# One-token attention with a feed-forward branch on one core: w2 split evenly, products in halves of a tile, one matmul for the queries, one store for the result

## The chip, the cores and the metric

One core of one Trainium2 chip runs the kernel. The metric is the device time of one execution in microseconds (us), lower is better; a time is the median of several runs. The profiler gives a span, from the first to the last instruction, which is a little shorter than the device time of the same execution. Engines are called by the short names of the profile: PE is TensorE (its weight loads are PEld), DVE is VectorE, ACT is ScalarE, POOL is GpSimd, SP is SyncE. A name with a q (SPq, ACTq) is the engine's instruction queue, which issues DMAs.

## The reference

Four tokens, one per batch entry, each go through layer normalisation, then through an attention with cached keys and values and, beside it, through a feed-forward block. Both results are added to the input. Everything is float32.

```python
B, Sq, D = 4, 1, 512;  H, Sk, Dh = 32, 4096, 128;  F = 1792
def _A_ref(x, k_cache, v_cache, wq, wo):          # caches: (B, H, Sk, Dh)
    q = (x @ wq).reshape(B, Sq, H, Dh).transpose(0, 2, 1, 3)
    scores = jnp.einsum("bhqd,bhkd->bhqk", q, k_cache) * (Dh ** -0.5)
    p = jax.nn.softmax(scores, axis=-1)
    o = jnp.einsum("bhqk,bhkd->bhqd", p, v_cache)
    return o.transpose(0, 2, 1, 3).reshape(B, Sq, H * Dh) @ wo
def _B_ref(x, w1, w2):
    return jnp.einsum("bsf,fd->bsd", jax.nn.silu(jnp.einsum("bsd,df->bsf", x, w1)), w2)
xn = _layernorm(x)
return x + _A_ref(xn, k_cache, v_cache, wq, wo) + _B_ref(xn, w1, w2)
```

The two caches hold 268 MB each. They are read once; wq and wo are 8.4 MB each, w1 and w2 3.7 MB each.

## The kernel before

**Tiles.** The caches are cut into T = 32 tiles each: a tile is one batch entry b and G = 4 heads, in SBUF as 128 partitions by R = 128 rows of Dh = 128 numbers (65,536 bytes a partition, 8.4 MB). Each head takes 32 partitions, and each partition 128 consecutive positions of the cache. Two buffers (`k_t`) hold K tiles, one (`v_t`) holds a V tile. The buffers are used for other things at both ends: the first `k_t` serves as scratch for x and w1, the first `v_t` holds wq; at the end `k_t` also takes the last V tile and then w2, and `v_t` takes wo. All loads are issued by SP, in order, so that a load that must wait for its buffer holds up those behind it.

**The head** (lines 84 to 283). x is normalised; the feed-forward's hidden layer (w1, SiLU) is computed on PE and ACT and turned so that the hidden units lie on the partitions (`ht_sb`). The hidden layer has 1792 = 14 x 128 units. The kernel treats them as FC = 13 full pieces of 128 units on 128 partitions and FX = 4 pieces of HP = 32 units on 32 partitions (`hp_x`, `h_x`, `hx_sb`). The hidden units are spread out with zeros between them (`OS` = 8 columns each) so that a later matmul fills 32 output partitions. Then q is computed from wq (L245, L259) into `q_h`, heads on the partitions. `queries(n)` (L270) spreads the queries of four heads over the 128 partitions with four matmuls of 32 rows each, once for every four tiles.

**The loop** runs over the 32 tiles i (L364 to L386). For each tile:

- `products` (L285), called for each quarter of STEP = 32 rows: DVE multiplies K by the query, in place (L291); POOL adds the upper half of each row to the lower (L295), for POOL_ROWS = 32 rows of a quarter, in the last quarter for 16.
- `sums` (L302): DVE adds up the rows: those that POOL halved (L307) and those that it left whole (L306).
- `maxima` (L309): DVE finds the greatest score of each head with two reductions, two transposes of 32x32 blocks and one multiply by the scale (L317).
- `softmax` of the tile before (L321): four exponentials on ACT.
- `values` of the tile before (L330): 32 matmuls on PE, in the trace 64 instructions, of the probabilities with V.
- `heads_out` of the tile before (L345): ACT copies the result from PSUM (L349), DVE multiplies it by a mask (L352) and adds four columns into one (L356), PE adds it into the row of all heads (L357).

`tc.issue_after` holds the next tile's first products behind the maxima, and the queries' matmuls behind the V matmuls. The scheduler of the language sets the semaphores; each engine runs its instructions in the order of the program.

**The end** (L389 to L450). SP issues wo in two loads and w2 in pieces, cut at the numbers W2_CUTS. w2's 13 full pieces go to 128 partitions, in four loads with 7, 4, 1 and 1 rows of w2 for each; the other 128 rows of w2 go to 32 partitions, four rows each, in four loads of 64 KB to every fourth partition (L402). The last tile's `softmax`, `values` and `heads_out` follow. The heads' results are divided by the sums of the exponentials (L418), turned (L423, L428) and multiplied with wo, 32 matmuls in the loop at L437, which goes on with w2's first seven pieces and the four small ones. ACT copies these sums to SBUF (L441). `accumulate` (L155 to L161) adds them, and the products with w2's other pieces, into `acc`, where x already is: four matmuls each, one for 128 of the 512 output columns, into 32 partitions each. DVE copies `acc` (L447), and two DMAs, one issued by SP and one by ACT (L450), store 8 rows of 128 numbers each.

Of the kernel before, what the change touches and what calls it, by code (L numbers as in the profile page):

```python
# [20 lines left out]


@with_exitstack
def kernel(
# [67 lines left out]
    h_x = scratch[:, 5 * D + DC * F : 5 * D + DC * F + HP]  # L92
# [12 lines left out]
    nc.gpsimd.memset(h_x, 0.0)  # L105
    nc.vector.memset(xpad, 0.0)
    p_t = const.tile([P, R, G], F32, name="p_t")
    nc.gpsimd.memset(p_t, 0.0)
# [37 lines left out]
        own, pick.rearrange("p (r g) -> p r g", r=NR), axis=AX, op=ALU.add  # L146
    )


    OS = PH // B  # L150
    fold = const.tile([P, B, OS], F32, name="fold")
    nc.gpsimd.memset(fold, 0.0)
    nc.vector.tensor_copy(fold[:, :, 0], pick[:, :B])

    def accumulate(lhsT, rhs, start=False, stop=False):  # L155

        for j in range(D // P):
            nc.tensor.matmul(  # L158
                acc[PH * j : PH * (j + 1), :], lhsT, rhs[:, j * P : (j + 1) * P],
                start=start, stop=stop,  # L160
            )  # L161

    accumulate(fold[:B].rearrange("p b s -> p (b s)"), x_sb, start=True)


    nmean = const.tile([B, 1], F32, name="nmean")
# [26 lines left out]

    hp = ps_s.tile([P, FT * P], F32, name="sm")
    hp_x = ps_s.tile([P, HP], F32, name="sm")
    w1_f = w1_t[:, :, : FC * P].rearrange("p c (m f) -> p c f m", f=FC)
    w1_x = w1_t[:, :, FC * P :].rearrange("p c (m f) -> p c f m", f=FX)  # L200
# [13 lines left out]
    for j in range(4):  # L214
        rows, n = slice(32 * j, 32 * j + B), FN[j] * P
        nc.scalar.activation(h_sb[rows, :n], hp[rows, :n], AF.Silu)
        nc.scalar.activation(h_x[rows, :], hp_x[rows, :], AF.Silu)
    hx_ps = ps_q.tile([HP, FX, B], F32, name="q_ps")
    nc.tensor.matmul(  # L219
        hx_ps, h_x, ident.rearrange("p (j m) -> p j m", j=FX)[:, :, :B], start=True, stop=True  # L220
    )
    hx_sb = const.tile([HP, FX, B], F32, name="hx_sb")
    nc.vector.tensor_copy(hx_sb, hx_ps)  # L223
    ht_ps = ps_s.tile([P, FT, 4, B], F32, name="sm")
    for t in range(FT):
        nc.tensor.matmul(
# [5 lines left out]
    ht_sb = const.tile([P, FT, 4, B, OS], F32, name="ht_sb")  # L232
    nc.gpsimd.memset(ht_sb, 0.0)
    nc.vector.tensor_copy(ht_sb[:, :, :, :, 0], ht_ps)
    hT = [ht_sb[:, t, j] for j in range(4) for t in range(FN[j])]


    NM = H // G // 4
    qp = ps_s.tile([P, G * Dh], F32, name="sm")
# [23 lines left out]
                start=True, stop=True,  # L263
            )
    q_h = const.tile([P, B, Dh], F32, name="q_h")
    nc.vector.tensor_copy(q_h, qh_ps)  # L266

    q_ps, vs, st = {}, {}, {}

    def queries(n):  # L270

        t = ps_q.tile([P, B, Dh], F32, name="q_ps")
        for g in range(G):
            rows = slice(g * PH, (g + 1) * PH)
            k = g * PH + PH // 4 * (n // NM) + n % NM
            nc.tensor.matmul(  # L276
                t[rows].rearrange("p b d -> p (b d)"),
                ident[rows, k : k + 1].to_broadcast([PH, PH]),
                q_h[rows].rearrange("h b d -> h (b d)"),
                start=True, stop=True,  # L280
            )
        for b in range(B):
            q_ps[n * B + b] = t[:, b, :]

# [23 lines left out]

    def maxima(i):  # L309

        nc.vector.tensor_reduce(m_t[:, :1], st[i], axis=AX, op=ALU.max)  # L311
        mt = small.tile([P, PH], F32, name="mt", bufs=1)
        nc.vector.transpose(mt, m_t)  # L313
        gm = small.tile([P, 1], F32, name="gm", bufs=1)
        nc.vector.tensor_reduce(gm, mt, axis=AX, op=ALU.max)
# [3 lines left out]
        return nb, nc.vector.transpose(nb, mb).ins  # L319

    def softmax(i, nb):  # L321
        s = st.pop(i)
        for g in range(G):
            rows = slice(g * PH, (g + 1) * PH)
            nc.scalar.activation(  # L325
                p_t[rows, :, g], s[rows, :], AF.Exp, bias=nb[rows, :1], scale=scale,
                accum_out=l_t[rows, i % B, i // B, g : g + 1],
            )

# [15 lines left out]
    def heads_out(i):  # L345

        h, b = i // B * G, i % B
        o_sb = small.tile([P, NR, Dh], F32, name="o_sb", bufs=1)
        nc.scalar.activation(  # L349
            o_sb.rearrange("p r d -> p (r d)"), o_ps, AF.Copy  # L350
        )
        nc.vector.tensor_tensor(  # L352
            o_sb, o_sb, own[:, :, None].to_broadcast([P, NR, Dh]), op=ALU.mult
        )
        o_1 = small.tile([P, Dh], F32, name="o_1", bufs=1)
        nc.vector.tensor_reduce(o_1, o_sb.rearrange("p r d -> p d r"), axis=AX, op=ALU.add)  # L356
# [34 lines left out]
    w2_x = w2_t[:HP, FC * D : (FC + FX) * D]  # L391
    w2_t = w2_t[:, : FC * D].rearrange("p (f n) -> p f n", f=FC)
    src_x = w2[FC * P :].rearrange("(p e) n -> p (e n)", p=HP)
    for t, w, n, cuts in ((wo_t, wo, H, WO_CUTS), (w2_t, w2[: FC * P], FC, W2_CUTS)):
# [19 lines left out]
        )  # L414
    rl = const.tile([H, B], F32, name="rl")
    nc.vector.reciprocal(rl, ls_ps)
    o_row = const.tile([H, B, Dh], F32, name="o_row")
# [4 lines left out]
    for n in range(NQ):  # L422
# [4 lines left out]
    ot = const.tile([P, H, B], F32, name="ot")  # L427
    nc.vector.tensor_copy(ot, ot_ps.rearrange("p b c -> p c b"))  # L428

    part = ps_q.tile([P, D], F32, name="q_ps")  # L430
    nc.vector.memset(part, 0.0)
    rows = [(ot[:, c, :], wo_t[:, c, :]) for c in range(H)]
    rows += [(hT[f][:, :, 0], w2_t[:, f, :]) for f in range(W2_CUTS[0])]
    rows += [(hx_sb[:, e, :], w2_x[:, e * D : (e + 1) * D]) for e in range(FX)]
    for c, (a, w) in enumerate(rows):
        j = 32 * (c % 4)
        nc.tensor.matmul(  # L437
# [1 line left out]
        )  # L439
    part_sb = small.tile([P, NR * Dh], F32, name="o_sb", bufs=1)  # L440
    nc.scalar.activation(part_sb, part, AF.Copy)  # L441
    accumulate(fold.rearrange("p b s -> p (b s)"), part_sb)
    for f in range(W2_CUTS[0], FC):
        accumulate(hT[f].rearrange("p b s -> p (b s)"), w2_t[:, f, :], stop=(f == FC - 1))

    res = small.tile([P, P], F32, name="s")
    nc.vector.tensor_copy(res, acc)  # L447
    of = of.rearrange("b (j n) -> j b n", j=D // P)
    for k, eng in enumerate((nc.sync, nc.scalar)):
        eng.dma_start(of[2 * k : 2 * k + 2], res[k * P // 2 : (k + 1) * P // 2 : OS, :])  # L450


# [30 lines left out]
```

## Time and profile before

| what | value |
|---|---|
| device time, median of 3 runs | 1306.87 us (1306.11 to 1307.1) |
| device time of the profiled execution | 1306.47 us |
| span of the profiled execution | 1304.5 us |
| DVE busy | 974.5 us (75%), 541 instructions |
| POOL busy | 511.5 us (39%), 145 instructions |
| PE busy (matmuls) | 357.1 us (27%), 2518 instructions |
| ACT busy | 92.8 us (7%) |
| bytes moved by DMA | 561.42 MB, 430 GB/s over the span |
| mean granted clock of PE | 0.629 |

The busy tenths of the page cut the span into 40 slices of 32.6 us; a 9 stands for 90% or more. A group of the page is one line of the code on one engine: the shapes out and in, the count, the total and the mean, and then how long the engine stood idle just before those instructions and what ended it. A timeline row gives the start, the length, the engine, the line, the operation and the count of merged instructions. A stretch gives busy time by engine in the order PE, PEld, DVE, ACT, POOL, then the clock granted to PE, the busy share of the 16 DMA engines and the rate in GB/s. Shares of short stretches can pass 1, because a packet is booked where it ends.

### The profile page before, as it was taken

The page shows a single profiled execution, that of the slowest core. Times are in us where ns is not written, and L with a number is a line of the kernel's source. Part 1 is how long each engine was busy: PE and PEld are TensorE (multiplying, and loading weights), DVE is VectorE, ACT ScalarE, POOL GpSimd, SP SyncE. Part 2 cuts the span into 40 slices and gives each one's busy share as a digit, 9 for nine tenths or more (in the row PEclk, how much of TensorE's full clock was granted, in tenths as well). Part 3 has the DMA queues.
Part 4 walks back from the last instruction along what each step waited for, and adds up shares of the span by engine and source line. Part 5 has one row for each costly group of instructions (what it writes and reads, how often), then busy time and mean ns, then how long its engine had stood idle before and what let it go on. Part 6 is the DMA issues. An engine that isn't in the chain of part 4 may idle for free.

```text
span 1304.5 us, 6383 instructions
## 1 busy us (share of the span) xinstructions
PE 357.1 (27%) x2518; PEld 87.1 (7%) x2518; DVE 974.5 (75%) x541; ACT 92.8 (7%) x301; POOL 511.5 (39%) x145
## 2 busy tenths in 40 slices
PE   4321232221123321133322132332123232212227
PEld 1000000000000000000000000000000000000001
DVE  1499777887777797777797777788777779777770
ACT  1010000000000000000000000000000000000000
POOL 0255333444333444332444433344433344433340
PEclk9655666655666665666665566665566666566668
DMA  9999999999999999999999999999999999999997
GB/s 402 449 421 446 422 445 424 443 426 442 427 437 432 435 434 434 435 432 437 432 433 436 432 435 432 437 430 439 430 439 428 441 426 443 424 444 425 440 423 327
DMA packets 10490, 561.42 MB, mean 430 GB/s; under 512 B 1192, under 2 KB 1208, under 8 KB 1468
## 3 DMA queue, kind: packets, MB, share of 16 engines
q1 hardware_dynamic: 10450, 561.01, 99.4%
q8 instruction: 20, 0.33, 0.1%
q14 instruction: 10, 0.08, 0.0%
q10 hardware_dynamic: 10, 0.00, 0.0%
HBM read 561.00 MB, written 0.01 MB: 430 GB/s over the span
## 4 chain that ended last, share of the span: by engine, by line
DMA 73%; PE 18%; DVE 7%; POOL 1%; issue 0%; SPq 0%; ACT 0%; POOLq 0%; DVEq 0%; ACTq 0%
DMA v_t<-in_A_v_cache_dram 53%; PE o_ps L336 17%; DMA k_t<-in_A_k_cache_dram 15%; DVE k_t L291 4%; DMA k_t<-in_B_w_dram 3%; DVE s L307 2%; DMA v_t<-in_A_wq_dram 2%; POOL k_t L295 1%; PE sm L245 1%; DVE s L306 1%; PE q_ps L437 0%; PE acc L158 0%; DVE m_t L311 0%; DVE mt L313 0%; ACT o_sb L441 0%
## 5 line engine op out<-in xcount | busy, mean ns | idle before, releaser
L295 POOL TENSOR_TENSOR k_t<-k_t 128x2048 f32<-128x2048 f32 (+1 forms) x128 | 508.6, 3984 | 745.6 <-DVE k_t L291 745.6
L291 DVE TENSOR_TENSOR k_t<-k_t,q_ps 128x4096 f32<-128x4096 f32 x128 | 562.3, 4413 | 222.9 <-DMA k_t<-in_A_k_cache_dram 222.9
L336 PE MATMUL o_ps<-v_t,p_t 128*16 128x512 f32 x1984 | 286.0, 741 | 824.6 <-DMA v_t<-in_A_v_cache_dram 824.6
L307 DVE TENSOR_REDUCE s<-k_t 128x32 f32<-128x2048 f32 (+1 forms) x128 | 257.6, 2013 | 11.5 <-POOL k_t L295 11.5
L336 PEld LDWEIGHTS o_ps<-v_t,p_t 128*16 128x16 f32 x1984 | 66.6, 113 | 1026.1 <-issue 945.9
L349 ACT ACTIVATE o_sb<-o_ps 128x512 f32<-128x512 f32 x32 | 19.1, 597 | 1097.0 <-issue 1081.4
L306 DVE TENSOR_REDUCE s<-k_t 128x16 f32<-128x2048 f32 x32 | 72.8, 2276 | 0.0
L325 ACT ACTIVATE p_t<-s,nb 32x128 f32<-32x128 f32 x128 | 66.5, 519 | 16.9 <-DVE nb L319 13.4
L352 DVE TENSOR_TENSOR o_sb<-o_sb,own 128x512 f32<-128x512 f32 x32 | 21.8, 680 | 28.1 <-ACT o_sb L349 27.9
L357 PE MATMUL o_all<-o,w_t 128*32 128x128 f32 x64 | 15.6, 332 | 88.4 <-DVE o L356 88.4
L356 DVE TENSOR_REDUCE o<-o_sb 128x128 f32<-128x512 f32 x32 | 32.7, 1023 | 3.2
L325 ACT ACTIVATION_READ_ACCUMULATOR p_t<-s,nb 32x1 f32 x128 | 25.5, 199 | 0.0
L357 PEld LDWEIGHTS o_all<-o,w_t 128*32 128x32 f32 x64 | 4.8, 116 | 117.8 <-DVE o L356 117.8
L447 DVE COPY s<-acc 128x128 f32<-128x128 f32 x1 | 0.3, 292 | 14.8 <-PE acc L158 14.8
L336 PE MATMUL o_ps<-k_t,p_t 128*16 128x512 f32 x64 | 9.0, 724 | 7.6 <-DMA k_t<-in_A_v_cache_dram 7.6
L245 PE MATMUL sm<-v_t,xpad 128*32 128x512 f32 x64 | 9.9, 786 | 1.0 <-DMA v_t<-in_A_wq_dram 1.0
L311 DVE TENSOR_REDUCE m_t<-s 128x1 f32<-128x128 f32 x32 | 9.1, 284 | 1.1
L223 DVE COPY hx_sb<-q_ps 32x16 f32<-32x16 f32 x1 | 0.2, 163 | 12.4 <-PE q_ps L219 12.4
L319 DVE STREAM_TRANSPOSE nb<-mb 128x32 f32<-128x32 f32 x32 | 6.8, 211 | 3.3
L437 PE MATMUL q_ps<-v_t,ot 128*4 128x512 f32 x64 | 8.8, 701 | 0.4 <-DVE ot L428 0.4
L276 PE MATMUL q_ps<-q_h,ident 32*32 32x512 f32 x64 | 8.5, 599 | 0.8 <-DVE q_h L266 0.8
L255 DVE COPY o_sb<-sm 128x512 f32<-128x512 f32 x1 | 0.7, 691 | 10.6 <-PE sm L245 10.6
(85 smaller groups left out, 77.1 us busy)
## 6 DMA issues: line engine op xcount, KB each, us to landing
v_t<-in_A_wo_dram SPq DMA_DIRECT2D x2, 4096.0 KB, 25.4
k_t<-in_B_w_dram SPq DMA_DIRECT2D x1, 3584.0 KB
k_t<-in_B_w_dram SPq DMA_DIRECT2D x1, 1792.0 KB
k_t<-in_B_w_dram SPq DMA_DIRECT2D x1, 1024.0 KB, 27.2
k_t<-in_A_k_cache_dram SPq DMA_DIRECT2D x32, 48.2
k_t<-in_B_w_dram SPq DMA_DIRECT2D x2, 256.0 KB, 13.6
v_t<-in_A_v_cache_dram SPq DMA_DIRECT2D x31, 28.9
k_t<-in_B_w_dram SPq DMA_DIRECT2D x4, 64.0 KB
```

The costliest lines, as they stand in the source:

```text
L245: nc.tensor.matmul(qp[32 * j : 32 * j + 32, :], xpad[:, c, a : a + PH], wq_t[:, c, n * G * Dh : (n + 1) * G * Dh], start=(m == 0 and c == ...
L291: nc.vector.tensor_tensor(k[:, a:z, :], k[:, a:z, :], q[:, None, :].to_broadcast([P, STEP, Dh]), op=ALU.mult)
L295: nc.gpsimd.tensor_tensor(k[:, a:v, :half], k[:, a:v, :half], k[:, a:v, half:], op=ALU.add)
L306: nc.vector.tensor_reduce(s[:, v:z], k[:, v:z, :], axis=AX, op=ALU.add)
L307: nc.vector.tensor_reduce(s[:, a:v], k[:, a:v, :half], axis=AX, op=ALU.add)
L311: nc.vector.tensor_reduce(m_t[:, :1], st[i], axis=AX, op=ALU.max)
L325: nc.scalar.activation(p_t[rows, :, g], s[rows, :], AF.Exp, bias=nb[rows, :1], scale=scale, accum_out=l_t[rows, i % B, i // B, g : g + 1],)
L336: last = nc.tensor.matmul(o[j : j + NR * G, :], p_t[:, rows, :].rearrange("p r g -> p (r g)"), v[:, rows, :].rearrange("p r d -> p (r d)") ...
L349: nc.scalar.activation(o_sb.rearrange("p r d -> p (r d)"), o_ps, AF.Copy)
L352: nc.vector.tensor_tensor(o_sb, o_sb, own[:, :, None].to_broadcast([P, NR, Dh]), op=ALU.mult)
L356: nc.vector.tensor_reduce(o_1, o_sb.rearrange("p r d -> p d r"), axis=AX, op=ALU.add)
L357: nc.tensor.matmul(o_all[:, b, :], w_t[:, W0 - h : W0 - h + H], o_1, start=False, stop=(i == T - 1))
```

## The change

- STEP is 64 instead of 32 rows, so that `products` is called twice a tile; POOL halves 64 rows of the first half and 48 of the second. The halved and whole rows of a tile stay 112 and 16.
- q is multiplied by minus the scale when it is copied (`q_h`); the maxima become minima, and the multiply by the scale falls away. Nine DVE instructions a tile remain in the loop.
- `heads_out` multiplies and adds on POOL, in three instructions, instead of on DVE in two.
- `queries` is one matmul with 128 rows, against a table `spread`, which POOL writes at the head with two copies.
- The hidden layer is 14 full pieces of 128 units; the 32-partition pieces, the zeros between columns and the products with them fall away. w2 is loaded in four loads to all 128 partitions, with 7, 4, 2 and 1 rows each. None of them waits for an earlier load any more (before, the last three did, because of the number of loads in flight).
- `accumulate` writes 4 partitions in each of the four blocks of 32, instead of 32. The result is brought into 4 partitions by four copies, on DVE and ACT in turn, and stored by one DMA of SP.
- Some tiles share buffers: `o_row`, `ot` and `res` take those of `o_sb` and `s`.

```diff
-STEP = 32
-POOL_ROWS = 32
-POOL_ROWS_LAST = 16
+STEP = 64
+POOL_ROWS = 64
+POOL_ROWS_LAST = 48
-W2_CUTS = (7, 11, 12)
+W2_CUTS = (7, 11, 13)
...
-    FX = 4
-    HP = 32
-    FC = (F - HP * FX) // P
+    FC = F // P
...
-                acc[PH * j : PH * (j + 1), :], lhsT, rhs[:, j * P : (j + 1) * P],
+                acc[32 * j : 32 * j + B, :], lhsT, rhs[:, j * P : (j + 1) * P],
...
-        for j in range(FX):
-            nc.tensor.matmul(
-                hp_x[32 * j : 32 * j + B, :], xnT[:, c, :], w1_x[:, c, j, :],
-                start=(c == 0), stop=(c == DC - 1),
-            )
...
-    nc.vector.tensor_copy(q_h, qh_ps)
+    nc.vector.tensor_scalar_mul(q_h, qh_ps, -scale)
+    spread = const.tile([P, H // G, G, PH], F32, name="spread")
+    rows = ident.rearrange("p (g j m) -> p j g m", g=G, j=4)
+    for m in range(NM):
+        nc.gpsimd.tensor_copy(
+            spread.rearrange("p (j m) g i -> p m j g i", m=NM)[:, m],
+            rows[:, :, :, m, None].to_broadcast([P, 4, G, PH]),
+        )
...
-        for g in range(G):
-            rows = slice(g * PH, (g + 1) * PH)
-            k = g * PH + PH // 4 * (n // NM) + n % NM
-            nc.tensor.matmul(
-                t[rows].rearrange("p b d -> p (b d)"),
-                ident[rows, k : k + 1].to_broadcast([PH, PH]),
-                q_h[rows].rearrange("h b d -> h (b d)"),
-                start=True, stop=True,
-            )
+        nc.tensor.matmul(
+            t.rearrange("p b d -> p (b d)"),
+            spread[:, n].rearrange("p g i -> p (g i)"),
+            q_h.rearrange("h b d -> h (b d)"),
+            start=True, stop=True,
+        )
...
-        nc.vector.tensor_reduce(m_t[:, :1], st[i], axis=AX, op=ALU.max)
+        nc.vector.tensor_reduce(m_t[:, :1], st[i], axis=AX, op=ALU.min)
...
-        mb = small.tile([P, PH], F32, name="mb", bufs=1)
-        nc.vector.tensor_scalar_mul(mb, gm.to_broadcast([P, PH]), -scale)
...
-        nc.vector.tensor_tensor(
+        nc.gpsimd.tensor_tensor(
             o_sb, o_sb, own[:, :, None].to_broadcast([P, NR, Dh]), op=ALU.mult
         )
-        o_1 = small.tile([P, Dh], F32, name="o_1", bufs=1)
-        nc.vector.tensor_reduce(o_1, o_sb.rearrange("p r d -> p d r"), axis=AX, op=ALU.add)
+        nc.gpsimd.tensor_tensor(o_sb[:, :2, :], o_sb[:, :2, :], o_sb[:, 2:, :], op=ALU.add)
+        o_1 = o_sb[:, 2, :]
+        nc.gpsimd.tensor_tensor(o_1, o_sb[:, 0, :], o_sb[:, 1, :], op=ALU.add)
...
-            if z == W2_CUTS[0]:
-                for q in range(4):
-                    nc.sync.dma_start(w2_x[q::4, :], src_x[q::4, :])
...
-    rows += [(hT[f][:, :, 0], w2_t[:, f, :]) for f in range(W2_CUTS[0])]
-    rows += [(hx_sb[:, e, :], w2_x[:, e * D : (e + 1) * D]) for e in range(FX)]
+    rows += [(hT[:, f, :], w2_t[:, f, :]) for f in range(W2_CUTS[0])]
...
-    res = small.tile([P, P], F32, name="s")
-    nc.vector.tensor_copy(res, acc)
-    of = of.rearrange("b (j n) -> j b n", j=D // P)
-    for k, eng in enumerate((nc.sync, nc.scalar)):
-        eng.dma_start(of[2 * k : 2 * k + 2], res[k * P // 2 : (k + 1) * P // 2 : OS, :])
+    res = small.tile([P, NR * Dh], F32, name="o_sb", bufs=1)[:B]
+    for j in range(D // P):
+        src, dst = acc[32 * j : 32 * j + B, :], res[:, j * P : (j + 1) * P]
+        if j % 2 == 0:
+            nc.vector.tensor_copy(dst, src)
+        else:
+            nc.scalar.activation(dst, src, AF.Copy)
+    nc.sync.dma_start(of, res)
```

More of the change, by code (lines that the diff above doesn't have):

```diff
@@ L104 @@
     nc.gpsimd.memset(h_sb, 0.0)
-    nc.gpsimd.memset(h_x, 0.0)
     nc.vector.memset(xpad, 0.0)
@@ L147 @@
     )
[L150 to L153, printed above, removed]
     def accumulate(lhsT, rhs, start=False, stop=False):
@@ L158, in accumulate @@
             nc.tensor.matmul(
-                acc[PH * j : PH * (j + 1), :], lhsT, rhs[:, j * P : (j + 1) * P],
+                acc[32 * j : 32 * j + B, :], lhsT, rhs[:, j * P : (j + 1) * P],
                 start=start, stop=stop,
             )
-    accumulate(fold[:B].rearrange("p b s -> p (b s)"), x_sb, start=True)
+    accumulate(ident[:B, :B], x_sb, start=True)
     nmean = const.tile([B, 1], F32, name="nmean")
@@ L197 @@
     hp = ps_s.tile([P, FT * P], F32, name="sm")
-    hp_x = ps_s.tile([P, HP], F32, name="sm")
-    w1_f = w1_t[:, :, : FC * P].rearrange("p c (m f) -> p c f m", f=FC)
-    w1_x = w1_t[:, :, FC * P :].rearrange("p c (m f) -> p c f m", f=FX)
+    w1_f = w1_t.rearrange("p c (m f) -> p c f m", f=FC)
     for c in range(DC):
@@ L216 @@
         nc.scalar.activation(h_sb[rows, :n], hp[rows, :n], AF.Silu)
-        nc.scalar.activation(h_x[rows, :], hp_x[rows, :], AF.Silu)
-    hx_ps = ps_q.tile([HP, FX, B], F32, name="q_ps")
-    nc.tensor.matmul(
-        hx_ps, h_x, ident.rearrange("p (j m) -> p j m", j=FX)[:, :, :B], start=True, stop=True
-    )
-    hx_sb = const.tile([HP, FX, B], F32, name="hx_sb")
-    nc.vector.tensor_copy(hx_sb, hx_ps)
     ht_ps = ps_s.tile([P, FT, 4, B], F32, name="sm")
@@ L231 @@
         )
[L232 to L235, printed above, removed]
+    hT = const.tile([P, FC, B], F32, name="hT")
+    for j in range(4):
+        z = F0[j] + FN[j]
+        nc.vector.tensor_copy(hT[:, F0[j] : z, :], ht_ps[:, : FN[j], j, :])
     NM = H // G // 4
@@ L325, in softmax @@
             nc.scalar.activation(
-                p_t[rows, :, g], s[rows, :], AF.Exp, bias=nb[rows, :1], scale=scale,
+                p_t[rows, :, g], s[rows, :], AF.Exp, bias=nb[rows, :1], scale=-1.0,
                 accum_out=l_t[rows, i % B, i // B, g : g + 1],
@@ L390 @@
     w2_t = kpool.tile([P, R, Dh], F32, name="k_t").rearrange("p r d -> p (r d)")
-    w2_x = w2_t[:HP, FC * D : (FC + FX) * D]
     w2_t = w2_t[:, : FC * D].rearrange("p (f n) -> p f n", f=FC)
-    src_x = w2[FC * P :].rearrange("(p e) n -> p (e n)", p=HP)
-    for t, w, n, cuts in ((wo_t, wo, H, WO_CUTS), (w2_t, w2[: FC * P], FC, W2_CUTS)):
+    for t, w, n, cuts in ((wo_t, wo, H, WO_CUTS), (w2_t, w2, FC, W2_CUTS)):
         w = w.rearrange("(p f) n -> p f n", p=P)
@@ L416 @@
     nc.vector.reciprocal(rl, ls_ps)
-    o_row = const.tile([H, B, Dh], F32, name="o_row")
+    o_row = small.tile([P, NR, Dh], F32, name="o_sb", bufs=1)[:H]
     nc.vector.tensor_tensor(
@@ L426 @@
         )
-    ot = const.tile([P, H, B], F32, name="ot")
+    ot = small.tile([P, P], F32, name="s").rearrange("p (c b) -> p c b", b=B)
     nc.vector.tensor_copy(ot, ot_ps.rearrange("p b c -> p c b"))
```

11 lines of the change are left out of this document (4 added, 7 removed).

## The prediction

> **What bounds the kernel now.** I began with the page: the busy tenths by slice, the DMA queues, the chain's shares, and the group of the widest VectorE instruction.
>
> ```profile
> DVE  1499777887777797777797777788777779777770
> ...
> DMA  9999999999999999999999999999999999999997
> GB/s 402 449 421 446 422 445 424 443 426 442 427 437 432 435 434 434 435 432 437 432 433 436 432 435 432 437 430 439 430 439 428 441 426 443 424 444 425 440 423 327
> ...
> q8 instruction: 20, 0.33, 0.1%
> ...
> L291 DVE TENSOR_TENSOR k_t<-k_t,q_ps 128x4096 f32<-128x4096 f32 x128 | 562.3, 4413 | 222.9 <-DMA k_t<-in_A_k_cache_dram 222.9
> ```
>
> The DMA row is full in every slice but the last, at some 434 GB/s, while VectorE, the busiest engine, stands idle 222.9 us waiting for K. So the loop is a stream of 561 MB that nothing interrupts. Next the timeline of one tile from the middle, to see how far the engines are from interrupting it:
>
> ```profile
> 563.93 0.33 SPq L83 DMA_DIRECT2D v_t<-in_A_v_cache_dram  x1
> ...
> 564.35 0.38 SPq L83 DMA_DIRECT2D k_t<-in_A_k_cache_dram  x1
> ...
> 573.67 8.75 DVE L291 TENSOR_TENSOR k_t<-k_t,q_ps 128x4096 f32<-128x4096 f32 x2 [7.24 <-DMA k_t<-in_A_k_cache_dram]
> ...
> 593.10 8.87 PE L336 MATMUL o_ps<-v_t,p_t 128*16 128x512 f32 x64 [25.98 <-DMA v_t<-in_A_v_cache_dram]
> ...
> 600.23 1.21 DVE L307 TENSOR_REDUCE s<-k_t 128x16 f32<-128x1024 f32 x1
> ...
> 602.02 0.33 SPq L83 DMA_DIRECT2D v_t<-in_A_v_cache_dram  x1
> ```
>
> The K load issued at 564.35 stands behind a V load that takes until 592.96, so K could be issued some 28 us later and the stream would not notice. A V load is issued 9 us after the one before landed, while about 19 us of K is queued: 10 us of slack. VectorE works from 573.67 to 601.44 on a tile (27.8 us), and a pair of tiles lasts 38.6 us. Nothing in the loop sets the end but the stream's own rate, and this change keeps its bytes. What can move is the end. Its timeline:
>
> ```profile
> 1281.23 0.60 ACT L349 ACTIVATE o_sb<-o_ps 128x512 f32<-128x512 f32 x1 [16.96 <-issue]
> ...
> 1281.86 0.69 DVE L352 TENSOR_TENSOR o_sb<-o_sb,own 128x512 f32<-128x512 f32 x1 [17.10 <-ACT o_sb L349]
> 1282.58 1.02 DVE L356 TENSOR_REDUCE o<-o_sb 128x128 f32<-128x512 f32 x1
> ...
> 1286.43 8.76 PE L437 MATMUL q_ps<-v_t,ot 128*4 128x512 f32 x64 [0.38 <-DVE ot L428]
> 1295.71 1.90 PE L437 MATMUL q_ps<-k_t,ht_sb 128*4 128x512 f32 x14 [0.52 <-DMA k_t<-in_B_w_dram]
> 1297.54 1.04 PE L437 MATMUL q_ps<-k_t,hx_sb 32*4 32x512 f32 x8
> 1298.69 0.60 ACT L441 ACTIVATE o_sb<-q_ps 128x512 f32<-128x512 f32 x1 [16.86 <-PE q_ps L437]
> ...
> 1301.14 0.29 DVE L447 COPY s<-acc 128x128 f32<-128x128 f32 x1 [14.77 <-PE acc L158]
> 1301.46 0.59 SPq L450 DMA_DIRECT2D out_dram<-s  x1
> 1301.47 1.42 ACTq L450 DMA_DIRECT2D out_dram<-s  x1
> ```
>
> PE reaches the first piece of w2 only 0.5 us before it has landed: TensorE's serial work and the stream arrive together. The last view is the stretches of half a microsecond there (length, busy of each engine, clock, DMA share, GB/s):
>
> ```profile
> 1295.00:1295.50 0.50, 0.19 (x4) 0.00 (x0) 0.00 (x0) 0.00 (x0) 0.00 (x0) 1.00 0.83 340
> ...
> 1297.50:1298.00 0.50, 0.50 (x11) 0.10 (x8) 0.00 (x0) 0.00 (x0) 0.00 (x0) 1.00 0.25 102
> ...
> 1299.50:1300.00 0.50, 0.50 (x24) 0.50 (x20) 0.00 (x0) 0.00 (x0) 0.00 (x0) 1.00 0.12 45
> ```
>
> The share falls away over 5 us instead of at once: some DMA engines end early, a few late. The landing marks that each of the 16 leaves behind every load say the same: the spread between first and last is 0.74 us at the first load and 4.92 us at the last V (1267.16 and 1272.08). The last piece of w2 lands at 1300.55.
>
> **The change part by part**, against the profiled execution (span 1304.5, time 1306.47, which is 0.40 below the median 1306.87).
>
> *Halves of a tile, nine VectorE instructions, the scale moved into q, the maximum's multiply dropped: 0.* The elements are the same: 128 rows multiplied, 112 halved by GpSimd as before (64+48 against 3x32+16). From K's landing: two multiplies of 2 x 4.33 (17.4); GpSimd's first half 9.05, from 8.8 to 17.9; sum of 64 halved rows 4.4 (22.3); 16 whole rows 2.2 (24.5); GpSimd's 48 rows, 4.52 + 2.37 less one start of 0.2, end at 24.6; their sum 3.4 (28.0). That is 0.2 later than now, with 28 us of cover; without cover it would cost 32 x 0.2 = 6 us. The 0.18 us multiply (L317) and 1.7 us (L352, L356) leave VectorE, which is idle anyway: 0.
>
> *Queries by one matmul: 0.* The nearest row is L130, 128x512, two instructions, 1.92 us, against 1.06 for the four quarters now. It follows the V matmuls, whose last one already released the next V load, and 26 us of waiting for V hide it. The two GpSimd copies that build the spread table run near 3 us, long before q (45 us).
>
> *The head without the extra w2 rows and the padded w1 product: 0.* It ends before wq lands (31.25).
>
> *heads_out on GpSimd: in the loop 0, at the end +1.1.* In the loop its three instructions follow the tile's last half and have about 10 us until the next. At the end they stand in the chain. GpSimd's rows: 128x2048 4.524, 128x1024 2.367, so 2.106 ns an element and 0.21 a start: 512, 256 and 128 elements take 1.29 + 0.75 + 0.48 = 2.52, plus three hops of 0.12 (VectorE to GpSimd at 1004.63): 2.88 against 1.77 now (1281.83 to 1283.60). Ends: +0.2 (896 elements, no starts but one hop) and +3.0 (twice the rate an element, since these are other shapes). I take +1.1, whose rows are the same operation.
>
> *164 TensorE instructions fewer: the last V lands 0.45 earlier.* 34 products of the padded rows and 48 of the queries go, each a weight load and a matmul. In the trace, instruction blocks of 16 KB arrive every 76 us or so, and the first, ninth and seventeenth (32.9, 597.0, 1178.0) are followed by steps of about 1.0 us in the spread of landings; the eighteenth (1255.7) raises it from 4.41 to 4.92 just ahead of the last V. 164 instructions at some 134 a tile of 38.6 us are 47 us, so this block comes after the last V: -0.45. Ends: 0, and -0.9 if other engines' blocks also miss the slowest one. [...]
>
> *w2 even over the partitions.* wo's 64 matmuls now end at 1295.2; they will end at 1295.2 + 1.1 - 0.45 = 1295.85. The first piece (1295.66) has landed by then: the wait of 0.48 is absorbed. 14 matmuls take 1.90 where 22 took 2.91: -1.01. ScalarE as before. Then 64 instead of 56 matmuls of L158, at 1.78/56 = 0.032: +0.25. Together TensorE ends 1.1 - 0.45 - 0.48 - 1.01 + 0.25 = -0.59, at 1300.5. The stream: each of the four 64 KB loads is marked by 8 DMA engines only, the latest ones among them, and takes these 1.2 us (a packet of 8 KB is 0.31); spread over 16 the last piece lands 0.6 earlier, near 1300.0, and its 8 matmuls would end at 1300.3. So TensorE decides, by 0.2.
>
> *Result in 4 partitions: +0.9.* All four copies write one tile, and each waits for the one before across engines. A copy of 128 columns on VectorE is 0.29; on ScalarE 0.25 (between 4x32 at 0.17 and 4x384 at 0.48); three hops of 0.04: 1.20 against 0.29. Ends: +0.3 (pairs side by side) and +1.4 (ScalarE at 0.48).
>
> *One store: -0.36.* ScalarE's store needs 1.42 us of issue and its mark comes at 1303.50, SyncE's at 1303.14. Without ScalarE's the end follows SyncE's. Ends: 0 and -0.6 (a plain load's issue is 0.33, not 0.59).
>
> **Sum**: -0.59 + 0.9 - 0.36 = -0.05: 1306.4 by the profiled execution, 1306.8 as a median.
>
> **The rivals.**
> *The end chain is longer (slower).* GpSimd's three instructions in the last heads_out at twice the rate: +1.9 on the sum, 1308.7, and 1309.0 with the copies at their upper end. Any excess over 0.05 makes it slower than before; for it: no row has GpSimd at these shapes; against: two shapes on one line.
> *The blocks' move gains nothing (a little slower).* If another DMA engine is then as late, V lands at 1272.08 as now, and the sum is 1306.8 + 0.45 = 1307.3. For it: ten blocks of 8 KB of the other engines' instructions also arrive, on engines that the trace does not name. Against: at the load after V the second-latest mark is 0.53 us ahead of the last.
> *The end is shorter (faster).* Copies in pairs, the blocks' -0.9 and a 0.33 us issue: -1.1 or so, 1305.7. No less than 1305.3: the last piece's landing near 1300 and the store's 3 us stand behind any work.
> *The halves stop overlapping (slower).* If GpSimd waited for both multiplies, a tile would take 17.4 + 15.7 + 10 + 1 = 44 us against 38.6, and the loop 32 x 5.5 = 176 us more: 1483. It decides once a tile passes 38.6. Against it: GpSimd starts at 578.22 inside VectorE's 573.67 to 582.42 today.
> *VectorE bound the loop after all (faster).* 1.9 us fewer a tile would give 32 x 1.9 = 61 us: 1246. Against: its 222.9 us of idling for K.
>
> **How the numbers follow.** Forecast, the trade at the end: 60 in 100, 1305.8 to 1308.0. Blocks without gain 12, longer end 13, shorter end 11, no overlap 2, VectorE 2. Within 0.2% (2.6 us, about what a measurement tells from no change) lie the first two, 8 of the longer and 8 of the shorter end: 0.88. Slower: 0.07, 5 of the longer end and the lost overlap. Faster: 0.05, 3 of the shorter end (something at the head or the stream that I have not seen) and VectorE. The predicted time is 1306.8. The bounds of the parts, joined as independent, give -1.2 and +2.1: 1305.5 to 1308.9; 0.2 more below for the spread of runs.
>
> **What would show it.** Pairs of V landings still 38.6 us apart; VectorE idle for K, more than 222.9 us by some 60; GpSimd's last three at 2.5 us; no wait of TensorE for w2's first piece; four copies in a row before the store; the spread of landings under 4.9 at the last V. Wrong would be a gap in the DMA row within the loop, an end chain that waits for w2's last piece, or copies side by side.

## The result and the profile after

The changed kernel takes 1309.89 us, the median of 11 runs (1308.99 to 1311.55); the kernel before, on the same chip, 1306.87 (11 runs, 1306.11 to 1308.33). The ratio is 1.0025, with a 95% interval of 1.0016 to 1.0035: slower by 3.0 us. The profiled execution took 1310.83 us with a span of 1309.1, which is 4.4 and 4.6 us more than before's. Its page first:

```profile
DMA  9999999999999999999999999999999999999997
GB/s 403 445 431 435 431 435 437 427 441 425 437 429 435 433 431 435 431 435 429 437 431 433 433 435 431 435 431 437 431 433 433 433 431 441 425 439 427 437 423 300
...
q8 instruction: 19, 0.31, 0.1%
...
L270 DVE TENSOR_TENSOR k_t<-k_t,q_ps 128x8192 f32<-128x8192 f32 x64 | 553.1, 8684 | 298.4 <-DMA k_t<-in_A_k_cache_dram 298.4
```

The loop is still a stream: no gap in the DMA row, and VectorE idles for K 298.4 us, 75 more than before. One tile pair from the middle, as a timeline:

```profile
555.78 8.84 PE L314 MATMUL o_ps<-v_t,p_t 128*16 128x512 f32 x64 [25.42 <-DMA v_t<-in_A_v_cache_dram]
...
575.01 17.29 DVE L270 TENSOR_TENSOR k_t<-k_t,q_ps 128x8192 f32<-128x8192 f32 x2 [9.90 <-DMA k_t<-in_A_k_cache_dram]
583.78 15.53 POOL L274 TENSOR_TENSOR k_t<-k_t 128x4096 f32<-128x4096 f32 x2 [15.97 <-DVE k_t L270]
...
594.50 9.95 PE L314 MATMUL o_ps<-v_t,p_t 128*16 128x512 f32 x64 [26.23 <-DMA v_t<-in_A_v_cache_dram]
```

GpSimd starts on the first half while VectorE multiplies the second, and the V matmuls of two tiles start 38.72 us apart, where it was 38.64 before: over 32 tiles that is some 2.5 us. Nothing in the loop interrupts the DMA. Then the end:

```profile
1274.33 9.67 PE L314 MATMUL o_ps<-k_t,p_t 128*16 128x512 f32 x64 [6.55 <-DMA k_t<-in_A_v_cache_dram]
...
1284.83 1.04 POOL L330 TENSOR_TENSOR o_sb<-o_sb,own 128x512 f32<-128x512 f32 x1 [17.55 <-ACT o_sb L327]
1285.95 0.72 POOL L333 TENSOR_TENSOR o_sb<-o_sb 128x256 f32<-128x256 f32 x1
1286.75 0.45 POOL L335 TENSOR_TENSOR o_sb<-o_sb 128x128 f32<-128x128 f32 x1
...
1288.66 2.07 PE L396 MATMUL sm<-o_sb,up 32*128 32x128 f32 x8 [0.77 <-DVE o_sb L391]
...
1291.11 9.80 PE L409 MATMUL q_ps<-v_t,s 128*4 128x512 f32 x64 [0.38 <-DVE s L401]
...
1300.74 1.89 PE L409 MATMUL q_ps<-k_t,hT 128*4 128x512 f32 x14
...
1305.40 0.28 DVE L423 COPY o_sb<-acc 4x128 f32<-4x128 f32 x1 [14.34 <-PE acc L147]
...
1306.33 0.27 ACT L425 ACTIVATE o_sb<-acc 4x128 f32<-4x128 f32 x1 [0.35 <-DVE o_sb L423]
1306.63 0.29 SPq L426 DMA_DIRECT2D out_dram<-o_sb  x1
```

The V matmuls and the turning in the kernel before:

```profile
1272.12 8.98 PE L336 MATMUL o_ps<-k_t,p_t 128*16 128x512 f32 x64 [7.57 <-DMA k_t<-in_A_v_cache_dram]
...
1284.92 1.12 PE L423 MATMUL sm<-o_row,up 32*128 32x128 f32 x8 [0.86 <-DVE o_row L418]
```

Two things differ from before at once. The last V matmuls start at 1274.33, and before they started at 1272.12; the stream of the same bytes is 2.2 us late when the end begins. And TensorE's pieces are longer, though their shapes are the old ones: the turning (L396) 2.07 where it took 1.12, wo 9.80 where it took 8.76. The table puts the span's 4.6 us together from such rows, beside the prediction's terms:

| term | predicted | profiled execution |
|---|---|---|
| last V lands (1272.08 before, 1274.29 after) | -0.45 | +2.21 |
| V matmuls, last tile (9.11 to 9.82) | 0 | +0.71 |
| heads_out on GpSimd (1.79 to 2.42, and 0.05 more before it) | +1.1 | +0.68 |
| its matmul, the division and the turning (2.78 to 3.86) | 0 | +1.08 |
| wo and w2's first pieces (12.26 to 11.58) | -1.49 | -0.68 |
| `accumulate` | +0.25 | +0.26 |
| copies | +0.9 | +0.91 |
| the store and what follows it | -0.36 | -0.57 |
| sum | -0.05 | +4.6 |

TensorE's part is a matter of its clock. The two windows below are from before and from after (length, busy of PE, PEld, DVE, ACT, POOL, granted clock, DMA share, GB/s), while wo is multiplied:

```profile
1290.00:1294.00 4.00, 4.00 (x40) 0.84 (x36) 0.00 (x0) 0.00 (x0) 0.00 (x0) 1.00 0.96 402
```

```profile
1290.00:1297.00 7.00, 6.62 (x36) 1.53 (x39) 0.29 (x1) 0.00 (x0) 0.00 (x0) 0.52 0.95 399
```

In 4 us at clock 1.00 before ran 40 matmuls; in 7 us at 0.52 after ran 36, a few of the turning's among them. By the clock records the half-rate stretch of this part of the end lasted 3.41 us in before's profiled execution and 10.24 in after's. How much of that belongs to the change, and what slows the stream, is for the experiments.

### The profile page after: what moved, and what is told of

It is laid out like the page before. It is cut to its first block, busy times and chain, and to the rows that moved or that the text cites. A ratio compares the mean times of both kernels' runs of the same rounds, so it can differ in the third digit from the quotient of the medians.

```text
span 1309.1 us, 6031 instructions
## 1 busy us (share of the span) xinstructions
PE 353.7 (27%) x2436; PEld 89.2 (7%) x2436; DVE 910.0 (70%) x319; ACT 93.0 (7%) x299; POOL 571.5 (44%) x176
## 4 chain that ended last, share of the span: by engine, by line
DMA 74%; PE 22%; POOL 1%; DVE 1%; issue 0%; ACT 0%; SPq 0%; POOLq 0%; ACTq 0%; DVEq 0%
DMA v_t<-in_A_v_cache_dram 65%; PE o_ps L314 20%; DMA k_t<-in_A_v_cache_dram 4%; DMA k_t<-in_A_k_cache_dram 4%; DMA v_t<-in_A_wq_dram 2%; POOL k_t L274 1%; PE q_ps L409 1%; PE sm L218 1%; DVE k_t L270 1%; DVE s L286 0%; PE sm L396 0%; PE acc L147 0%; POOL o_sb L330 0%; POOL o_sb L333 0%; DVE o_sb L391 0%
## 5 line engine op out<-in xcount | busy, mean ns | idle before, releaser
L270 DVE TENSOR_TENSOR k_t<-k_t,q_ps 128x8192 f32<-128x8192 f32 x64 | 553.1, 8684 | 298.4 <-DMA k_t<-in_A_k_cache_dram 298.4
L274 POOL TENSOR_TENSOR k_t<-k_t 128x4096 f32<-128x4096 f32 x64 | 497.4, 7795 | 541.7 <-DVE k_t L270 541.7
L286 DVE TENSOR_REDUCE s<-k_t 128x64 f32<-128x4096 f32 x64 | 248.7, 3886 | 14.3 <-POOL k_t L274 12.5
L330 POOL TENSOR_TENSOR o_sb<-o_sb,own 128x512 f32<-128x512 f32 x32 | 33.2, 1039 | 168.3 <-ACT o_sb L327 168.3
L336 PE MATMUL o_all<-o_sb,w_t 128*32 128x128 f32 x64 | 15.3, 327 | 100.5 <-POOL o_sb L335 87.5
L333 POOL TENSOR_TENSOR o_sb<-o_sb 128x256 f32<-128x256 f32 x32 | 23.1, 722 | 2.5
L335 POOL TENSOR_TENSOR o_sb<-o_sb 128x128 f32<-128x128 f32 x32 | 14.5, 454 | 2.5
L336 PEld LDWEIGHTS o_all<-o_sb,w_t 128*32 128x32 f32 x64 | 4.8, 118 | 129.3 <-POOL o_sb L335 129.3
L409 PE MATMUL q_ps<-v_t,s 128*4 128x512 f32 x64 | 9.8, 780 | 0.4 <-DVE s L401 0.4
L255 PE MATMUL q_ps<-q_h,spread 128*128 128x512 f32 x16 | 9.0, 643 | 0.9 <-DVE q_h L239 0.9
```

The source lines that it names most:

```text
L270: nc.vector.tensor_tensor(k[:, a:z, :], k[:, a:z, :], q[:, None, :].to_broadcast([P, STEP, Dh]), op=ALU.mult)
L274: nc.gpsimd.tensor_tensor(k[:, a:v, :half], k[:, a:v, :half], k[:, a:v, half:], op=ALU.add)
L286: nc.vector.tensor_reduce(s[:, a:v], k[:, a:v, :half], axis=AX, op=ALU.add)
L330: nc.gpsimd.tensor_tensor(o_sb, o_sb, own[:, :, None].to_broadcast([P, NR, Dh]), op=ALU.mult)
L333: nc.gpsimd.tensor_tensor(o_sb[:, :2, :], o_sb[:, :2, :], o_sb[:, 2:, :], op=ALU.add)
L336: nc.tensor.matmul(o_all[:, b, :], w_t[:, W0 - h : W0 - h + H], o_1, start=False, stop=(i == T - 1))
```

## The experiments

The first reading of the records behind the page was this. Each load is made of packets of 64 KB, one for each partition, on 16 DMA engines, 520 on each. In before's execution 8131 of the 8320 packets took 2418 ns (mean 2419.7). In after's, 4355 took 2421 and 1697 took 2428 (mean 2424.0). 520 x 4.3 ns is 2.2 us: the whole delay of the last V. So the question was why a packet of the same size takes longer. Halves with longer instructions, the run itself, another part of the change, and the place of the buffers in SBUF were the candidates.

**The kernel before, once more** (no edit), to see whether the packets' length is a matter of the execution.

> The kernel before, unchanged, looked at once more. Theory A (the halves of a tile lengthen the stream: the 64 KB packets of the changed kernel take 2421 ns in the median against 2418 before): packets at 2418 ns again, last V landed near 1272, time near 1306.9. Theory B (the slower stream of the changed kernel's profile belongs to the run and not to the change, and what the change costs lies behind the last V): the packets may as well be at 2421 ns here and the last V near 1274, time up to 1309.

One run: 1307.21, against 1306.57, the median of before's runs on that chip. Its packets took 2418 ns again, and the last V landed at 1271.80. So a second execution of before doesn't have the longer packets. What did differ from before's first profile is the end: the half-rate stretch was 6.83 us long instead of 3.41, with the turning at 2.04 and the V matmuls at 9.80, where they were 1.12 and 8.98. So the clock in the end varies from execution to execution of one and the same program.

**Halves alone in the kernel before**

```diff
-STEP = 32
-POOL_ROWS = 32
-POOL_ROWS_LAST = 16
+STEP = 64
+POOL_ROWS = 64
+POOL_ROWS_LAST = 48
```

> The kernel before with nothing but the halves (STEP 64, POOL 64 and 48 rows). Theory A: the stream slows as in the changed kernel, so +2.2 us, 1309.1, last V landed near 1274. Theory B: no change, 1306.9 within 0.4, last V near 1272.

1306.56 (11 runs), ratio 1.0 (0.9991 to 1.0009); packets 2418 ns; last V at 1271.75. The halves cost nothing, and they don't slow the stream. This part of the prediction went as written.

**The changed kernel with `heads_out` back on VectorE**

```diff
-        nc.gpsimd.tensor_tensor(
+        nc.vector.tensor_tensor(
             o_sb, o_sb, own[:, :, None].to_broadcast([P, NR, Dh]), op=ALU.mult
         )
-        nc.gpsimd.tensor_tensor(o_sb[:, :2, :], o_sb[:, :2, :], o_sb[:, 2:, :], op=ALU.add)
-        o_1 = o_sb[:, 2, :]
-        nc.gpsimd.tensor_tensor(o_1, o_sb[:, 0, :], o_sb[:, 1, :], op=ALU.add)
+        o_1 = small.tile([P, Dh], F32, name="o_1", bufs=1)
+        nc.vector.tensor_reduce(o_1, o_sb.rearrange("p r d -> p d r"), axis=AX, op=ALU.add)
```

> The changed kernel with heads_out on VectorE as before, two instructions. Theory A: the last heads_out is 0.6 us shorter and nothing else moves: 1309.3. Theory B: TensorE's gap between the last V matmuls and wo is 0.6 us shorter, which in some runs also keeps the clock at 1.00 or brings it back a step of 3.4 us earlier: 1309.3 down to 1307.5.

1309.16 (1308.92 to 1309.94), ratio 1.002 (1.0011 to 1.0029): 0.7 less than the changed kernel by the medians, and the rest of the loss stays. Last V at 1274.42, packets still 2421 and 2428. GpSimd's work isn't what slows the stream.

**The changed kernel with two tiles for the result and two stores**

```diff
-    res = small.tile([P, NR * Dh], F32, name="o_sb", bufs=1)[:B]
-    for j in range(D // P):
...
-    nc.sync.dma_start(of, res)
+    for k, eng in enumerate((nc.sync, nc.scalar)):
+        if k == 0:
+            res = small.tile([P, NR * Dh], F32, name="o_sb", bufs=1)[:B, : 2 * P]
+        else:
+            res = spread.rearrange("p n g i -> p (n g i)")[:B, : 2 * P]
+        for j in (2 * k, 2 * k + 1):
...
+        eng.dma_start(of[:, 2 * k * P : (2 * k + 2) * P], res)
```

> The changed kernel with the result in two tiles: VectorE copies the first 256 columns and SyncE stores them, ScalarE copies the others and stores them. Both theories: the four copies in a row (1.23 us) become two and two side by side (0.6), and ScalarE's store gives back some 0.3: 1309.5, 0.3 to 0.4 below the changed kernel. If the copies were hidden by something, no change: 1309.9.

1310.8 (6 runs, 1309.17 to 1311.65), ratio 1.0031 (1.0019 to 1.0042): the expected gain did not come. In its chain VectorE's first copy starts at 1303.69, and ScalarE's only at 1304.36, after both of VectorE's: with two tiles the copies still did not run side by side, so the four in a row were not undone. From the first copy to the end of the span it is 3.7 us in this execution, as in the changed kernel's (1305.40 to 1309.1). Six runs spread over 2.5 us can't price the second store more closely.

**The buffers' place.** The programs as built say where each tile lies. In the kernel before, the three large buffers start at bytes 28672, 94208 and 159744 of each partition, multiples of 256. In the changed one they start at 28192, 93728 and 159264, 32 bytes past a multiple of 256: the small tiles that are laid out ahead of them changed in number and size (`spread` came, `ht_sb`, `hx_sb`, `fold` and others went). The diff says nothing of this. The experiment adds a tile that nothing uses, of 56 numbers, so that the buffers start at 28416, which is 111 x 256:

```diff
+    pad = const.tile([P, 56], F32, name="pad")
+    nc.vector.memset(pad, 0.0)
     ident = const.tile([P, P], F32, name="ident")
```

> The changed kernel with an unused tile of 224 bytes a partition ahead of the tiles, so that the K and V buffers begin at byte 28416 of a partition, a multiple of 256, instead of 28192 (32 over one). Theory C (each DMA packet that begins off a multiple of 256 bytes takes some 3 ns more, and 520 packets a DMA engine make the last V 2.4 us late): packets at 2418 ns again, last V landed near 1271.8, time 1307.4, 2.4 below the changed kernel. Theory D (something else of the change slows the stream: the one matmul for the queries, the shared buffers): 2421 to 2424 ns and 1309.9 as it was.

1306.3 (11 runs, 1305.48 to 1308.52), ratio 1.0003 (0.9994 to 1.0012). The loss is gone. Of the packets 8159 took 2418 ns again, and the last V landed at 1271.37, 2.9 earlier than in the changed kernel.

**The same from the other side: the kernel before, moved by 32 bytes**, to 28704.

```diff
+    pad = const.tile([P, 8], F32, name="pad")
+    nc.vector.memset(pad, 0.0)
     ident = const.tile([P, P], F32, name="ident")
```

> The kernel before with nothing but an unused tile of 32 bytes a partition, so that the K and V buffers begin at byte 28704 instead of 28672 = 7 x 4096. Theory C: packets of 2421 and 2428 ns, last V landed near 1274.2, time 1309.0, 2.4 above the kernel before. Theory D: 1306.6, no change.

1309.64 (8 runs, 1309.28 to 1311.11), ratio 1.0027 (1.0017 to 1.0037). An unused tile of 32 bytes a partition costs as much as the whole change did. The packets are those of the changed kernel: 2421 and 2428 ns, mean 2424.1. Here is the same window of the loop in four kernels, with the columns as above, in the order before, after, after with the buffers moved to 28416, before with the buffers moved to 28704:

```profile
500.00:880.00 380.00, 101.36 (x676) 23.83 (x676) 298.16 (x160) 26.84 (x90) 158.90 (x40) 0.61 1.00 434
```

```profile
500.00:880.00 380.00, 99.21 (x664) 23.85 (x664) 279.11 (x90) 26.76 (x90) 177.54 (x50) 0.62 1.00 433
```

```profile
500.00:880.00 380.00, 97.24 (x664) 23.50 (x664) 278.08 (x90) 26.79 (x90) 177.67 (x50) 0.62 1.00 434
```

```profile
500.00:880.00 380.00, 97.43 (x676) 23.37 (x676) 299.62 (x160) 26.86 (x90) 159.00 (x40) 0.62 1.00 433
```

The rate follows the address and not the kernel: 434 GB/s at a multiple of 256, 433 at 32 past it. One in 434 over some 1240 us is 2.9 us, which a rounded figure can show only roughly; the starts of the last V matmuls show it better, first in the moved kernel after, then in the moved kernel before:

```profile
1271.41 8.35 PE L316 MATMUL o_ps<-k_t,p_t 128*16 128x512 f32 x64 [5.88 <-DMA k_t<-in_A_v_cache_dram]
...
1284.20 2.00 PE L398 MATMUL sm<-o_sb,up 32*128 32x128 f32 x8 [0.77 <-DVE o_sb L393]
```

```profile
1274.80 8.55 PE L338 MATMUL o_ps<-k_t,p_t 128*16 128x512 f32 x64 [6.34 <-DMA k_t<-in_A_v_cache_dram]
...
1294.26 3.62 PE L439 MATMUL q_ps<-v_t,ot 128*4 128x512 f32 x32 [0.55 <-DMA v_t<-in_A_wo_dram]
...
1298.57 1.90 PE L439 MATMUL q_ps<-k_t,ht_sb 128*4 128x512 f32 x14 [0.69 <-DMA k_t<-in_B_w_dram]
```

Before started them at 1272.12, after at 1274.33. In the last fence TensorE also waits for wo's second half and for w2, 0.55 and 0.69: with a late stream, the end is the DMA's again. Moving the buffers took the loss away in one kernel and brought it into the other: their start address is the cause. (The small tiles behind the unused one move too, but nearly all packets go to the large buffers.)

**The changed kernel at 28288, a multiple of 128 but not of 256** (a tile of 24 numbers).

> The changed kernel with 96 bytes of unused tile, so that the K and V buffers begin at byte 28288, 128 over a multiple of 256. [...] If a multiple of 128 is enough: 2418 ns and 1306.3.

1308.8 (11 runs, 1308.22 to 1310.53), ratio 1.002 (1.0011 to 1.0029). Most packets took between 2418 and 2426 ns, 2134 of them 2418, mean 2423.0, and the last V landed at 1273.74, 2.4 behind the kernel moved to a multiple of 256, where 32 past it costs 2.9. So a multiple of 128 was not enough here. But the time lies below the 1309.64 and 1309.89 of the two kernels at 32 past, and the packets are not theirs: the cost is some four fifths of that.

**A remedy for the clock that failed.** Three matmuls on data at hand were put behind the last V matmuls of the moved kernel, to keep TensorE busy until GpSimd is done.

```diff
-    values(T - 1)
+    warm = ps_s.tile([P, 512], F32, name="sm")
+    with tc.issue_after(values(T - 1)):
+        for _ in range(3):
+            nc.tensor.matmul(warm, ident, p_t.rearrange("p r g -> p (r g)"), start=True, stop=True)
     heads_out(T - 1)
```

> after_aligned with three more matmuls (128x512, their output unused) behind the last V matmuls, while ScalarE and GpSimd work on the last heads_out. Theory E (the end is long because TensorE waits 3.3 us for GpSimd, its granted clock falls to 0.5 and the turning and part of wo's matmuls run at half speed): the turning at 1.1 us instead of 2.1 and wo's 64 matmuls at 8.5 to 8.8 us in every run: 1 to 2 us below after_aligned, and its times no longer in two groups. Theory F (the clock follows something else, so the groups are of the run): no change, or up to 0.3 slower for the added matmuls.

1307.27 (11 runs, 1305.46 to 1308.09), ratio 1.0003 (0.9995 to 1.0012). The three ran 2.84 us from 1281.19, and the clock fell at 1287.0 all the same, to 1293.8; wo took 9.94. The edit also moved the matmuls of the sums (L384 in the changed kernel) behind the V matmuls, so it is no clean test of the gap: these matmuls now stand in the chain. That the gap in TensorE's work makes the clock fall was not shown.

**The even w2 alone in the kernel before**, with the buffers kept at 28672 by a tile of 16 numbers.

```diff
-W2_CUTS = (7, 11, 12)
+W2_CUTS = (7, 11, 13)
...
-    FX = 4
-    HP = 32
-    FC = (F - HP * FX) // P
+    FC = F // P
...
+    pad = const.tile([P, 16], F32, name="pad")
...
-            if z == W2_CUTS[0]:
-                for q in range(4):
-                    nc.sync.dma_start(w2_x[q::4, :], src_x[q::4, :])
```

> The kernel before with only w2 made even (14 full pieces, no 32-partition pieces, cuts 7, 11, 13), and the K and V buffers kept at a multiple of 256 bytes. By the sum of the prediction: 1.0 us less of matmuls behind wo, 0.25 more in the accumulation, and the last piece 0.6 earlier: 0.6 to 0.8 below the kernel before, 1305.9. If the even split brought nothing of its own (the waits elsewhere take it back): 1306.6.

1305.86 (11 runs, 1305.49 to 1306.58), ratio 0.9994 (0.9985 to 1.0003). The last piece of w2 lands at 1299.50, against 1300.55. The median is 0.6 below before's and the interval holds no change, so a gain is likely and not shown.

**The moved changed kernel with `heads_out` on VectorE** (both edits from above), to see what GpSimd costs once the stream is put right.

> after_aligned with heads_out on VectorE as before. Theory G (GpSimd's last heads_out costs its 0.6 us, 2.4 against 1.8, and beyond it half of the executions a longer stretch at clock 0.5): 0.6 below after_aligned's lower times, near 1305.7, and all runs in one group, as they were for after_vec_heads. Theory F (the two groups are of the run): 0.6 below in both groups, so still times near 1307.

1305.98 (11 runs, 1305.43 to 1306.9), ratio 0.9996 (0.9987 to 1.0004). Its end:

```profile
1284.16 1.15 PE L397 MATMUL sm<-o_sb,up 32*128 32x128 f32 x8 [0.77 <-DVE o_sb L392]
...
1285.69 8.80 PE L410 MATMUL q_ps<-v_t,s 128*4 128x512 f32 x64 [0.38 <-DVE s L402]
1295.14 1.89 PE L410 MATMUL q_ps<-k_t,hT 128*4 128x512 f32 x14 [0.64 <-DMA k_t<-in_B_w_dram]
```

Here the clock was at half rate for 3.41 us only, the turning took 1.15, wo 8.80, and TensorE had to wait 0.64 for w2. The medians differ by 0.3, which neither interval tells from nothing. With the work on GpSimd, four of eleven runs of the moved kernel lie at 1307.12 or above; with it on VectorE, none does. The pair of kernels at the address of the change shows the same: 5 of 11 at 1310.83 or above with GpSimd, none above 1309.94 with VectorE. Against a simple rule speaks the kernel before, which has VectorE there and two of 11 runs at 1308.2 and 1308.33; moved by 32 bytes, it has two of 8 at 1310.42 and 1311.11.

**The even w2 and one store from the old 16 rows**, in the kernel before.

```diff
-    for k, eng in enumerate((nc.sync, nc.scalar)):
-        eng.dma_start(of[2 * k : 2 * k + 2], res[k * P // 2 : (k + 1) * P // 2 : OS, :])
+    nc.sync.dma_start(of, res[::OS, :])
```

> before_even_w2 with one store of SyncE, 16 rows of 128 numbers, in place of the two of SyncE and ScalarE. As in the changed kernel, the end should follow the one issue: 0.3 to 0.5 below before_even_w2, 1305.4, and so below both kernels. If the issue of a strided store on SyncE costs as much as ScalarE's did: 1305.9, no change.

1305.63 (12 runs; eleven from 1305.08 to 1307.54, one of 1316.27), ratio 1.0 (0.9986 to 1.0013). It is the lowest median of all, 1.2 below before's on that chip (1306.82). The ratio is one of means and counts the execution of 1316.27, so it shows no gain: one is likely, and not shown. That execution is the profiled one, with a granted clock of 0.525 on average, so that no row of it can be set against the others.

## Why the prediction was wrong, point by point

**The step that failed: "Nothing in the loop sets the end but the stream's own rate, and this change keeps its bytes."** The first half held. From the second it was taken that the rate is kept too, and "164 TensorE instructions fewer: the last V lands 0.45 earlier" was then added to an unchanged stream. In the runs each packet took 4.3 ns of 2420 longer, through the buffers' start address, and the last V came 2.21 later instead of 0.45 earlier. None of the rivals held such a case: they were about the order of work, the length of instructions and the blocks of instructions, and none about where the buffers lie in SBUF. With the address put right, the kernel takes 1306.3, against a forecast of 1306.8; that this is so near is in part luck, since terms of the end were off both ways, as said below.

**The blocks' move** came, and its gain is likely. The eighteenth block arrived at 1278.4, after the last V, though 23 us later than before and not 47, and the spread of the landing marks at the last V was 4.49 instead of 4.92. With the buffers at a multiple of 256, the last V of the changed kernel lands at 1271.37, and at 1271.48 with `heads_out` on VectorE; with the block ahead of it, before's two executions and the halves alone have 1272.08, 1271.80 and 1271.75. That is 0.3 to 0.7, around the 0.45 of the sum, but the kernels differ in more than the block. These rows speak against the rival in which nothing is gained, and don't exclude it.

**TensorE's durations at the end: sizes taken from one execution.** The prediction took wo at 8.76, the turning at 1.12 and the V matmuls at 9.11 as properties of the kernel. They depend on where the half-rate stretch falls. In after's profiled execution this added 0.71 + 1.08 + 0.87 = 2.7 us (wo from its first matmul to w2's first: 9.63 instead of 8.76), and in the second execution of before part of the same is seen. So 4.6 is 2.2 of stream, 2.7 of clock and -0.3 of all the rest. At full clock at most 2.4 of the 2.7 could have been saved, because w2's last piece landed only at 1302.58 and eight matmuls of `accumulate` stand behind it. The clock's part belongs to that execution more than to the change: 6 of the 11 runs of the changed kernel lie between 1308.99 and 1309.89, which is 2.1 to 3.0 above before's median, about what the address alone cost in the kernel before (3.2). But the other five lie 1.8 higher on average, and of the changed kernel's runs at either address such times came in 9 of 22 with `heads_out` on GpSimd and in 0 of 22 with it on VectorE. So a part of it may well come with GpSimd's work; how, is open.

**Halves, queries, the head: 0.** Right, as far as tried. The halves were tried alone, and the others only within the moved kernel, whose median is 0.1 below before's. VectorE idles 75 us more for K, where some 60 was written.

**heads_out on GpSimd: +1.1.** Right in kind, too large: 0.68 in all. Its rows are 1.04, 0.72 and 0.45, 2.2 us together, where the line through the rows of other shapes gave 2.52. The medians put its price at 0.3 (moved, 1306.3 against 1305.98) and 0.7 (not moved), inside the bounds and not beyond the spread of the runs.

**w2.** TensorE's wait for the first piece was gone in after's execution, but by the slow clock: it reached w2 at 1300.74, and the piece had landed at 1298.18. Where the half-rate stretch was 3.41 us, the changed kernel still waited: 0.16 at 28288, and 0.64 at 28416 with `heads_out` on VectorE. 14 matmuls instead of 22 took 0.99 less (-1.01); 64 matmuls of `accumulate` 0.26 more (+0.25). The bound that the sum had 0.2 below it, the landing of the last piece, is reached in the moved kernel, where the last 24 matmuls start at 1299.58 and 1300.20, just after their pieces land (1299.53 and 1300.16).

**Copies: +0.9, and the store: -0.36.** Four in a row, +0.91; the store gave -0.57, near its bound of -0.6.

**The rivals.** "The end chain is longer" named the right sign and a price near the result (1308.7 to 1309.0; by its own terms the upper one is 1309.2), but its mechanism, GpSimd at twice the rate, did not happen: near by luck. "The halves stop overlapping" and "VectorE bound the loop after all" are excluded by the rows above, and "the blocks' move gains nothing" is made unlikely. "The end is shorter" is excluded by the copies in a row.

## What to carry to other kernels

Where DMA bounds a kernel, the start address of its large buffers belongs to what a change may alter: work it out for both kernels before predicting, and look at it again when small tiles ahead of it come or go. Here the kernel before took 1306.87 with its start at 28672 and 1309.64 at 28704, and the changed kernel 1306.3 at 28416, 1308.8 at 28288 and 1309.89 at 28192. An unused tile that moves the buffers tells in one run whether a small loss is the address or the change. And where TensorE's serial work makes the end, take its durations from several executions: in two of the kernel before, the half-rate stretch there was 3.41 and 6.83 us long, and the turning took 1.12 and 2.04.

## What the runs showed of the hardware

**The start of the buffers and the length of a packet.** With the large buffers at 28672 and at 28416, both multiples of 256, most packets of 64 KB took 2418 ns. With them 32 bytes past a multiple, at 28192 and at 28704, most took longer: in the changed kernel 3 to 4 or 10 to 11 ns, whatever their size (64 KB 2421 and 2428 against 2418 before, 32 KB 1216 and 1224 against 1213, 8 KB 313 and 320 against 309). So here it is a price for each packet and not for each byte. The source was the same, and the address in SBUF, the side that is written, had moved. At 28288, 128 past a multiple, the mean was 2423.0 against 2424.0 at 32 past and 2419.7 at 28672. Other starts were not tried, and what in the transfer takes the longer time is not shown.

**Why not from the start.** In the changed kernel 60 of the 64 packets that start in the first 20 us took 2418 ns, 91 of 198 between 50 and 80 us, and 24 of 270 between 110 and 150; before has 163 of 198 and 241 of 270 in the last two windows. So the surplus sets in within the first 110 us or so, and from then on most packets have it: of 661 that start between 600 and 700 us, 364 took 2421 ns and 150 took 2428, with some of 2419, 2420 and 2426 between. The kernel before moved by 32 bytes does the same. What delays the surplus was not tried and is open.

**The granted clock at the end.** Half-rate stretches near the end were 3.41 and 6.83 us long in two executions of before, 10.24 in after's and 6.83 in that of the moved kernel. These are one, two and three times 3.41. What decides how long the stretch is in a run, and why the changed kernels with GpSimd in the last `heads_out` show two groups of times some 1.8 us apart where those with VectorE show one, stays open. TensorE stands idle 3.26 us before its matmul of the last `heads_out` in the changed kernel, and 2.56 in the moved one with VectorE there. That the longer gap makes the clock fall was the author's guess and was not shown: the one attempt to fill it did not keep the clock up, and it was no clean test.
